# The first two blocks and the last make their output with w_out streaming past the activations; eight early chunks instead of ten; a new order of all operations

## The chip, the cores and the metric

One NeuronCore of a Trainium2 chip runs the program. The metric is device time in microseconds of one execution; a plain run's time and the span of the profiled execution are given side by side below.

## The reference, cut to what matters

A decayed linear attention over 4 batches, 8 heads, 768 tokens and head size 48 makes x (3072 tokens by 384), and a two-layer feed-forward with a cosine gate makes the output:

```python
for t in range(S):
    cur = np.einsum('bhd,bhe->bhde', u[None] * kt, vt)
    y[:, :, t] = np.einsum('bhd,bhde->bhe', rt, state + cur)
    state = w[None, :, :, None] * state + np.einsum('bhd,bhe->bhde', kt, vt)
x = y.transpose(0, 2, 1, 3).reshape(B * S, H * D)     # 3072 x 384
h = x @ w_in                                           # 3072 x 2048
g = h * np.cos(h)
out = g @ w_out                                        # 3072 x 384
```

## The kernel before

**Attention.** The tokens are cut into 24 chunks of 128 (six per batch). A chunk multiplies r and k by decay tables, makes scores, masks them, and multiplies by v and by the state of the chunk before. There are two forms. An *early* chunk transposes r and k on TensorE (`tr`, L970), makes scores (`mm_a`, L1089), the state product (`mm_z`, L1142) and x (`mm_x`, L1116 for the state's part and L1127 for the chunk's own). GpSimd (POOL) makes the product of r and k (L998), multiplies it by u (L1048) and decays k (L1006); VectorE (DVE) sums the products into `a` (L1054), masks (L1094) and splits x into a high and a low part (L1306); ScalarE (ACT) makes eight scaled diagonals from `a` (L1071). A *late* chunk has its transposes on DVE, stacks two half chunks and needs fewer matmuls (L1231, L1239, L1288). `EARLY = 10` says how many chunks take the early form.

**Feed-forward.** Six blocks of 512 tokens, and w_in's 2048 columns in 16 slices f, give 96 steps. A step is `h` (nine 512-column matmuls in a reduced fp32 format, high and low parts, L357), then on ACT and DVE in turn `qi` (L376), `rest` (L379), `cos` (L382), `gate` (L1399, writes h times cos back to PSUM), `gh` (L1402) and `gl` (L1405), then `o`: for each of three 128-wide parts of the output, three matmuls with a slice of w_out loaded as weights and the 512 tokens of gh or gl streaming (L373). The output so comes out transposed, three PSUM banks at a time, and DVE turns it back (L1431) into one SBUF tile `o` that is stored in pieces of 384 bytes (L1444, L1446). Blocks 0 and 1 take turns in groups of slices (`CUTS`), so that weights can be converted while they run; each group's end stores or adds to the output in DRAM (the adding DMA is issued by POOL). That makes twelve stored units: four for each of blocks 0 and 1, and one for each of the other four.

**Weights.** 32 pieces of w_in and w_out are read as 64-bit words and converted by ACT, DVE and POOL (L757, L765, L776, L787, L797, L804) during the first 170 us.

**Order.** Every operation is listed with its engine, a cost and the operations it waits for. `PLACE`, a table of numbers, gives each a rank; a planner walks the ranks with the costs and writes the instructions of each engine in the order that comes out. Where it sees a gap on TensorE ahead of the first `o`, it fills it with warm-up matmuls of 128 columns (L1462). Each engine's instructions run in that written order.

## Time and profile before

| | |
|---|---|
| Median of 3 runs | 500.93 us (500.54 to 501.88) |
| The profiled execution, its own time | 501.31 us |
| Its span in the profile | 499.5 us |
| TensorE (PE) busy | 486.6 us, 97% |
| VectorE (DVE) busy | 384.2 us, 77% |
| ScalarE (ACT) busy | 281.3 us, 56% |
| GpSimd (POOL) busy | 192.9 us, 39% |
| Share of the chain that ended last | PE 90%, DMA 3%, DVE 2% |

The span runs from the first to the last instruction that the profile recorded; the execution's own time is 1.8 us longer. PE counts as busy while any matmul is in its pipeline, and warm-up matmuls count as well, so 97% is not 97% of useful work.

### The profile page before, as it was taken

How to read it: one execution, taken by the hardware profiler on the slowest of the kernel's cores; microseconds unless marked ns; L12 is line 12 of the kernel's file. 1: busy time of each engine (PE TensorE's matmuls, PEld its weight loads, DVE VectorE, ACT ScalarE, POOL GpSimd, SP SyncE). 2: the span in 40 equal slices, each digit the busy share in tenths (PEclk: the TensorE clock that was granted, in tenths of full speed). 3: DMA queues.
4: the chain of work that ended last, by engine and by line, in shares of the span. 5: the costliest groups of instructions: out<-in, count | busy, mean ns of one | idle time of the engine just before them, and what ended most of it. 6: DMA issues, size and time to landing. Idle time of an engine off the chain costs nothing.

```text
span 499.5 us, 12059 instructions
## 1 busy us (share of the span) xinstructions
PE 486.6 (97%) x4676; PEld 393.8 (79%) x4676; DVE 384.2 (77%) x718; ACT 281.3 (56%) x644; POOL 192.9 (39%) x191
## 2 busy tenths in 40 slices
PE   9998999999999999999999999999999999999992
PEld 6887878878888878887878788887888888888881
DVE  6898999889899877777876895868857775665452
ACT  1987868566646655365565565565546545444440
POOL 6878342545756656543624242343505020000000
PEclk9999999999999999999999999999999999999998
DMA  7899647689897986477645466455533421110003
GB/s 140 172 186 171 140 140 193 155 143 156 147 207 113 184 109 118 62 169 141 132 115 141 126 143 145 132 128 142 130 77 92 142 80 33 33 31 2 1 0 70
DMA packets 150674, 59.19 MB, mean 118 GB/s; under 512 B 134223, under 2 KB 146513, under 8 KB 150609
## 3 DMA queue, kind: packets, MB, share of 16 engines
q1 hardware_dynamic: 136880, 53.24, 46.0%
q0 software_dynamic: 12672, 4.72, 9.8%
q8 instruction: 38, 0.62, 0.5%
q10 hardware_dynamic: 1056, 0.39, 0.3%
q14 instruction: 28, 0.22, 0.1%
HBM read 48.50 MB, written 9.44 MB: 116 GB/s over the span
## 4 chain that ended last, share of the span: by engine, by line
PE 90%; DMA 3%; DVE 2%; POOL 1%; SPq 1%; issue 1%; ACT 0%; DVEq 0%; POOLq 0%
PE psum L373 39%; PE psum L357 38%; PE psum L1288 3%; PE psum L1462 2%; PE psum L1231 2%; DMA out_dram<-o 1%; PE psum L1239 1%; DVE o L1431 1%; PE psum L1089 1%; PE psum L1127 1%; DMA early_v<-in_v_dram 1%; SPq L886 1%; PE psum L1116 1%; DMA early_k<-in_k_dram 1%; PE psum L970 1%
## 5 line engine op out<-in xcount | busy, mean ns | idle before, releaser
L373 PE MATMUL psum<-gh,w_out_hi 128*128 128x512 f32 x288 | 114.8, 399 | 0.9 <-DVE o L1431 0.9
L357 PE MATMUL psum<-xh,w_in_hi 128*128 128x512 f32 x288 | 114.1, 396 | 0.0
L357 PE MATMUL psum<-xh,w_in_lo 128*128 128x512 f32 x288 | 113.1, 393 | 0.0
L373 PE MATMUL psum<-gl,w_out_hi 128*128 128x512 f32 x288 | 113.1, 393 | 0.0
L373 PE MATMUL psum<-gh,w_out_lo 128*128 128x512 f32 x288 | 112.9, 392 | 0.0
L357 PE MATMUL psum<-xl,w_in_hi 128*128 128x512 f32 x288 | 112.7, 391 | 0.0
L1402 ACT CAST gh<-psum 128x512 fp32r<-128x512 f32 x96 | 56.0, 583 | 64.0 <-PE psum L373 33.8
L1405 DVE TENSOR_TENSOR gl<-psum,gh 128x512 fp32r<-128x512 f32 x96 | 65.6, 683 | 31.6 <-ACT gh L1402 30.9
L373 PEld LDWEIGHTS psum<-gh,w_out_hi 128*128 128x128 f32 x288 | 54.1, 188 | 14.5 <-DVE o L1431 0.9
L357 PEld LDWEIGHTS psum<-xh,w_in_hi 128*128 128x128 f32 x288 | 54.1, 188 | 13.1 <-issue 0.6
L373 PEld LDWEIGHTS psum<-gl,w_out_hi 128*128 128x128 f32 x288 | 54.1, 188 | 11.8
L357 PEld LDWEIGHTS psum<-xh,w_in_lo 128*128 128x128 f32 x288 | 54.1, 188 | 11.7
L357 PEld LDWEIGHTS psum<-xl,w_in_hi 128*128 128x128 f32 x288 | 54.1, 188 | 11.6
L373 PEld LDWEIGHTS psum<-gh,w_out_lo 128*128 128x128 f32 x288 | 54.1, 188 | 11.4 <-DVE w_out_lo L804 0.2
L1210 POOL TENSOR_TENSOR T<-T,k 48x512 f32<-48x512 f32 x28 | 37.2, 1328 | 55.5 <-ACT T L1196 29.0
L787 POOL TENSOR_TENSOR f<-f,raw 128x384 int32<-128x384 int32 x32 | 36.5, 1143 | 44.1 <-DVE f L776 26.3
L376 ACT ACTIVATE decT_r<-psum 128x512 int32<-128x512 f32 x41 | 24.5, 597 | 31.6 <-PE psum L357 31.4
L376 ACT ACTIVATE decT_k<-psum 128x512 int32<-128x512 f32 x41 | 24.4, 595 | 27.7 <-PE psum L357 26.9
L1196 ACT ACTIVATE T<-ident,a 128x128 f32<-128x128 f32 x112 | 37.1, 392 | 0.8 <-DVE a L1054 0.8
L1446 POOL DMA_DIRECT2D out_dram<-o x24 | 28.0, 1473 | 24.1 <-DVE o L1431 24.1
L379 DVE SCALAR_TENSOR_TENSOR decT_r<-psum,decT_r 128x512 f32<-128x512 f32 x41 | 28.0, 683 | 11.3 <-ACT decT_r L376 11.2
L379 DVE SCALAR_TENSOR_TENSOR decT_k<-psum,decT_k 128x512 f32<-128x512 f32 x41 | 28.0, 682 | 10.6 <-ACT decT_k L376 10.3
(161 smaller groups left out, 786.1 us busy)
## 6 DMA issues: line engine op xcount, KB each, us to landing
raw<-in_moe_w_out_dram SPq DMA_DIRECT2D x32, 384.0 KB, 3.5
raw<-in_moe_w_in_dram SPq DMA_DIRECT2D x32, 192.0 KB, 3.4
raw<-in_moe_w_in_dram SPq DMA_DIRECT2D x16, 384.0 KB, 3.8
out_dram<-o POOLq DMA_DIRECT2D x24, 192.0 KB, 5.3
raw<-in_k_dram SPq DMA_DIRECT2D x55, 80.0 KB, 3.0
raw<-in_r_dram SPq DMA_DIRECT2D x55, 80.0 KB, 2.4
out_dram<-o SPq DMA_DIRECT2D x22, 192.0 KB, 3.9
f<-in_k_dram SPq DMA_DIRECT2D x14, 192.0 KB, 3.6
```

The costliest lines, as they stand in the source:

```text
L357: nc.tensor.matmul(ph, a, b_, start=(i == 0), stop=(i == len(mm) - 1))
L373: nc.tensor.matmul(acc, a[:, ks], b_, start=(first and i == 0), stop=(last and i == 2))
L376: nc.scalar.activation(qi, ph, AF.Copy, scale=INV_2PI, bias=0.25)
L379: nc.vector.scalar_tensor_tensor(q, ph, INV_2PI, qi, op0=ALU.mult, op1=ALU.subtract)
L787: lambda: nc.gpsimd.tensor_tensor(ai(), ai(), cn(), op=ALU.add),
L1196: nc.scalar.activation(to, ident2[:, None, :].to_broadcast([P, 2, SUB]), AF.Copy, scale=ab()[:, h : h + 1])
L1210: nc.gpsimd.tensor_tensor(M_(n)[rows], by_head(rT)[rows], b_late[1]()[rows], op=ALU.mult)
L1231: nc.tensor.matmul(scores(n)[:, h, :], by_head(kT)[other(n), h, :], M_(n)[other(n), h, :], start=True, stop=True,)
L1288: nc.tensor.matmul(xv()[G * g : G * g + G, kk, tokens(n)], w_[rows, e0 : e0 + G], M_(n)[rows, h, :], start=g not in opened, stop=True, ski ...
L1402: nc.scalar.copy(gh(), ph())
L1405: nc.vector.tensor_tensor(gl(), ph(), f32(gh()), op=ALU.subtract)
L1446: nc.gpsimd.dma_start(dst, src, accum_op=ALU.add)
```

## The change

- For blocks 0 and 1 (`FLAT`) and for the last block, `o` is made the other way round: a 128-token slice of gh or gl is loaded as weights, and the 384 columns of w_out stream past. That is four tiles of three matmuls per step instead of three tiles of three. The output comes out with tokens in rows, so there is no transpose: ACT copies each finished tile (in the last block DVE and ACT in turn, and half of the last tile each), and it is stored in rows of 1536 bytes. The copies go to a ring `R_ob` of nine SBUF tiles instead of the single `o`.
- For blocks 0 and 1, `gate` writes to the SBUF tile q instead of PSUM, so gh and gl are made from SBUF, and h has two PSUM banks instead of three; the fourth accumulator takes the other.
- Eight early chunks instead of ten.
- A second pair of PSUM banks for the early transposes, a tile of its own for the mask `upper`, new costs for the planner, a new `PLACE`, and another count of warm-up matmuls.

```diff
-EARLY = 10
+EARLY = 8
 PLACE = (
-    14, 0, 7, 2, 3, 1, 12, 11, 6, 8, 5, 10, 15, 16, 24, 27, 40, 44, 22, 20, 28, 35, 13, 9, 31, 34, 25, 30, 33, 51, 42,
+    2, 0, 11, 3, 4, 5, 13, 21, 19, 9, 6, 12, 18, 20, 29, 37, 33, 36, 248, 7, 23, 26, 14, 10, 30, 27, 25, 46, 32, 57,
...
-        B_TR = [pair(0)]
+        B_TR = [pair(0), pair(6)]
...
+        FLAT = set(range(GRP))
+        R_ob = R_f + [Tile(t.ap[:, 0:DM], t.parts) for t in o_part]
...
-            ph, q, gh, gl = Buf(B_H), Buf(R_q), Buf(R_gh), Buf(R_gl)
+            flat_o, last = n in FLAT or n == NBLK - 1, n == NBLK - 1
+            ph, q, gh, gl = Buf(bank[3:5] if n in FLAT else B_H), Buf(R_q), Buf(R_gh), Buf(R_gl)
...
+            gb = q if n in FLAT else ph
+
+            def f_gate(ph=ph, q=q, gb=gb):
+                nc.vector.tensor_tensor(gb(), ph(), q(), op=ALU.mult)
...
-                acc_b[n, f0] = [Buf(B_ACC) for _ in range(NK)]
+                acc_b[n, f0] = [Buf([*B_ACC, bank[6 if last else 5]] if flat_o else B_ACC) for _ in range(nt if flat_o else NK)]
...
+                for t in range(nt):
+
+                    def o_(acc=acc[t], gh=gh, gl=gl, f=f, t=t, f0=f0, f1=f1):
+                        mm_o(acc()[:, 0:DM], gh(), gl(), f, t, f == f0, f == f1 - 1)
+
+                    oo = op(PE, s + 2.0 + 0.01 * t, 0.69, o_, [o6, (o7, 0.45), w_hi, (w_lo, 0.17)], [acc[t], gh, gl], line="o", mode=1)
+                    if f == f1 - 1:
+                        ob = Buf(R_ob)
+                        if not last:
+                            parts = ((ACT, SP if f0 == 0 else POOL, 0, 4),)
+                        elif t == nt - 1:
+                            parts = (DVE, SP, 0, 2), (ACT, ACT, 2, 4)
+                        else:
+                            parts = ((ACT if t % 2 else DVE, SP, 0, 4),)
...
-                    warm_up(int((o.gap - 0.1) / 0.057))
+                    cold = min(max(WARM_AT - (o.start - o.gap), 0.0), o.gap)
+                    warm_up(max(int(cold / 0.107 + (o.gap - cold - 0.1) / 0.057), 0))
```

`mm_o`, which was there for the fallback path, loads `a[:, ts]` (gh or gl) and streams `b_` (w_out):

```python
mm = ((g_hi, w_hi), (g_lo, w_hi), (g_hi, w_lo))
for i, (a, b_) in enumerate(mm):
    nc.tensor.matmul(acc, a[:, ts], b_, start=(first and i == 0), stop=(last and i == 2))
```

The new order moves instructions at three places that the prediction speaks of. The first is POOL near the program's start: the products r by k (L998, now L1007), the product by u (L1048, now L1057) and the decay of k (L1006, now L1015) of the first chunks. Before:

```order
L998 TENSOR_TENSOR f_109<-early_r_94,k_78 128x384
L998 TENSOR_TENSOR f_110<-early_r_95,k_77 128x384
L998 TENSOR_TENSOR f_105<-early_r_96,k_79 128x384
L1048 TENSOR_TENSOR f_110<-f_110,u_b 128x384
L1048 TENSOR_TENSOR f_105<-f_105,u_b 128x384
```

After:

```order
L1007 TENSOR_TENSOR f_110<-early_r_94,k_77 128x384
L1057 TENSOR_TENSOR f_110<-f_110,u_b 128x384
L1007 TENSOR_TENSOR f_105<-early_r_95,k_79 128x384
L1057 TENSOR_TENSOR f_105<-f_105,u_b 128x384
L1015 TENSOR_TENSOR k_79<-k_79,dec_k 128x2x4x48
```

The first chunk's product by u stood fourth, behind three products of r and k; it now stands second.

The second place is PE between the first `h` and the second (L357, now L362), where the early chunks' matmuls stand. Before, behind the first nine matmuls of h (the fourteen warm-ups L1462 and the rest are left out):

```order
L1142 MATMUL psum<-v_82,early_k_88 48x48 x8
L970 MATMUL psum<-ident,early_k_89 112x64 x8
...
L1089 MATMUL psum<-T 128x128 x8
L1116 MATMUL psum<-T,s 32x128 x16
L1127 MATMUL psum<-T,v_82 32x128 x16
L357 MATMUL psum<-xh,w_in_hi 128x512
L357 MATMUL psum<-xl,w_in_hi 128x512
```

After (L979, L1098, L1151, L1125 and L1136 are the new lines of tr, mm_a, mm_z and mm_x, and L369 is o in its new form):

```order
L1098 MATMUL psum<-T 128x128 x8
L979 MATMUL psum<-ident,early_k_90 112x64 x8
L979 MATMUL psum<-ident,early_r_97 112x64 x8
L369 MATMUL psum<-w_out_hi_68,gh_111 128x384
L369 MATMUL psum<-w_out_hi_68,gl_113 128x384
L369 MATMUL psum<-w_out_lo_69,gh_111 128x384
L1151 MATMUL psum<-early_v_91,early_k_90 48x48 x8
L362 MATMUL psum<-xh,w_in_hi 128x512
```

The first o now stands among the early chunks' matmuls, ahead of the second h; before, three more h stood ahead of the first o. Five early chunks' x (L1127) stood ahead of the first h before, four stand ahead of it now.

The third place is ACT at the end of the program, behind the last gh. Before:

```order
L1402 CAST gh_112<-psum 128x512
L1444 DMA out_dram<-o 32x16x96 x2
L1473 TENSOR_LOAD flag
```

After:

```order
L1414 CAST gh_112<-psum 128x512
L1436 COPY f_106<-psum 128x3x4x32
L1436 COPY f_108<-psum 128x3x2x32
L1447 DMA out_dram<-f_108 128x192
L1532 TENSOR_LOAD flag
```

ACT now copies the second tile and half of the fourth, and its store is one of half a tile (768 bytes a row); DVE copies the first, the third and the other half, and the three transposes that DVE had there are gone.

## Rows read from the trace of the kernel before

**Rows 1.** Windows: length, busy PE, PEld, DVE, ACT, POOL (instructions), clock, DMA, GB/s
```profile
0.00:8.43 8.43, 7.32 (x65) 5.27 (x66) 6.66 (x37) 1.49 (x2) 4.43 (x18) 1.00 0.64 119
8.43:20.00 11.57, 11.57 (x220) 9.76 (x220) 7.35 (x14) 6.83 (x22) 11.45 (x12) 1.00 0.90 179
20.00:56.98 36.98, 35.10 (x876) 29.64 (x870) 34.03 (x70) 31.49 (x90) 23.75 (x26) 1.00 0.95 172
56.98:107.12 50.14, 50.10 (x275) 40.26 (x271) 45.59 (x87) 34.44 (x72) 22.92 (x21) 1.00 0.69 161
109.47:490.50 381.03, 381.02 (x3254) 308.44 (x3254) 287.49 (x509) 206.45 (x459) 130.35 (x117) 1.00 0.51 106
```

**Rows 2.** Windows of the warm-up matmuls alone (L1462): PE and weight loads
```profile
0.00:20.00 20.00, 9.40 (x129) 8.37 (x129) 1.00 0.79 154
20.00:56.98 36.98, 1.52 (x21) 1.18 (x21) 1.00 0.95 172
```

**Rows 3.** Chain that ended last, from 408 us: start, us, what
```profile
412.68 1.93 PE psum L1288 x128
...
449.84 2.06 PE psum L373 x9
```

**Rows 4.** Timeline: start, us, engine, line: a change of matmul kind, and four transposes
```profile
414.54 0.19 PEld L373 LDWEIGHTS psum<-gh,w_out_hi 128*128 128x128 f32 x1
414.54 0.50 PE L373 MATMUL psum<-gh,w_out_hi 128*128 128x512 f32 x1
...
414.88 0.40 PE L373 MATMUL psum<-gh,w_out_lo 128*128 128x512 f32 x1
...
12.16 0.66 PE L590 MATMUL psum<-ident,decT_k 128*128 128x128 f32 x4
```

**Rows 5.** Chain from 44 us: one early chunk's five pieces, first and last
```profile
48.68 0.66 PE psum L970 x16
...
51.88 1.09 PE psum L1089 x16
```

**Rows 6.** Timeline of PE from 404.8 us: the first half of a late chunk
```profile
405.83 0.27 PE L1231 MATMUL psum<-T 48*64 48x64 f32 x2
...
406.91 0.50 PE L373 MATMUL psum<-gh,w_out_hi 128*128 128x512 f32 x1
```

**Rows 7.** Timeline near the start; in brackets idle time before, and what ended it
```profile
7.98 3.60 POOL L998 TENSOR_TENSOR f<-early_r,k 128x384 f32<-128x384 f32 x3 [2.93 <-DMA k<-in_k_dram]
...
13.48 1.00 DVE L1054 TENSOR_REDUCE a<-f 128x8 f32<-128x384 f32 x2
```

**Rows 8.** Timeline at 107 us, and PE's waits from 60 to 130 us
```profile
107.04 0.72 DVE L1431 STREAM_TRANSPOSE o<-psum 128x512 f32<-128x512 f32 x1 [1.76 <-DMA out_dram<-o]
...
PE psum L373 <- DVE o L1431: 0.9, 2, 0.5
```

**Rows 9.** Timeline at the end, and DMA issues there (median us to landing)
```profile
489.16 2.09 DVE L1431 STREAM_TRANSPOSE o<-psum 128x512 f32<-128x512 f32 x3 [1.67 <-PE psum L373]
490.10 0.39 PE L373 MATMUL psum<-gl,w_out_hi 128*128 128x512 f32 x1
491.28 0.98 ACTq L1444 DMA_DIRECT2D out_dram<-o  x2
...
out_dram<-o ACTq DMA_DIRECT2D x2, 192.0 KB, 5.2
```

**Rows 10.** Stores of out over the program, and a copy of 384 columns from PSUM
```profile
DMA to landing us min/median/max: 2.6/4.4/7.4
...
L594 ACT COPY dec_k<-psum x1: 482/482/482, 12.9 to 12.9; 128x384 f32<-128x384 f32 x1
```

**Rows 11.** Groups by line: two pieces of a step's chain
```profile
L376 ACT ACTIVATE decT_r<-psum 128x512 int32<-128x512 f32 x41 | 24.5, 597 | 31.6 <-PE psum L357 31.4
...
L379 DVE SCALAR_TENSOR_TENSOR decT_r<-psum,decT_r 128x512 f32<-128x512 f32 x41 | 28.0, 683 | 11.3 <-ACT decT_r L376 11.2
```

**Rows 12.** One line's instructions (ns min/median/max): w_in's low part, both operands in SBUF
```profile
L804 DVE TENSOR_TENSOR w_in_lo<-f,w_in_hi x16: 537/550/953, 33.7 to 157.3; 128x384 fp32r<-128x384 f32 x16
```

More of the change, by code (lines that the diff above doesn't have):

```diff
@@ L450 @@
         b_up = Buf(o_part[:1])
-        upper = o_room[:, 0:C].bitcast(I32)
+        upper = att.tile([P, C], I32, name="upper")
         warm = o_room[:, C : 2 * C].bitcast(BF16)[:, 0:P]
@@ L1438, with st @@
                 for a in range(P // G):
-                    def st(a=a, ob=ob, row=row, f0=f0, by=nc.scalar if last and a % 2 else nc.sync):
+                    def st(a=a, ob=ob, row=row, f0=f0):
                         dst = out[row : row + TB, a * NK * G : (a + 1) * NK * G].rearrange("(b i) e -> i b e", i=G)
```

108 lines of the change are left out of this document (68 added, 40 removed), and 192 rows, old and new, of the table PLACE.

## The prediction, made before the changed kernel was run

> **What bounds the kernel now.** I read the windows first, because they tell where TensorE (PE) has no room left. From 57 to 490 us it is busy in all but 0.04 of 50.14 us and 0.01 of 381.03 us of two long stretches, at a granted clock of 1.00, the upper of its two levels, 2.4 GHz [rows 1]; the 2.4 us between these two hold a wait, to which I come. So from 57 us on the time is the sum of PE's work, and only less work on PE makes it shorter. Before 57 us it is otherwise. The warm-up matmuls, which compute nothing, take 9.4 us of the first 20 and 1.5 of the next 37 [rows 2], and PE stands idle for 1.1 and 1.9 more, so some 14 of the first 57 us do no work. From 20 to 57 us VectorE (DVE) is busy 34.0 of 37.0 us: there DVE sets the pace. From 8.4 to 20 us it is busy only 7.35 of 11.57, waiting for its inputs, so that the start is held by the chain from the loads through GpSimd (POOL). After the last matmul, 490.10 + 0.39 = 490.49 us, the span of 499.5 us has 9.0 us left without PE [rows 9]. Three things can thus be gained or lost: work per matmul from 57 us on, the first 57 us, and the tail.
>
> **The change part by part.** The sum is made against the profiled execution, 501.31 us, with its span of 499.5.
>
> *The tail.* Now three transposes follow one another, the last ending at 489.16 + 2.09 = 491.25, four stores go out from 491.28, and the median to landing of those on ScalarE's queue is 5.2 us; the second on it goes out half of 0.98 us later, so the last lands at about 497, and 2.5 us remain to the span's end [rows 9]. The new form finishes its tiles one after another, so three of four are copied and two stored while PE still works. After the last matmul come half a copy, a store and the same 2.5 us. A copy of 384 columns takes 0.48 us [rows 10]; half takes between 0.24 and 0.48, I take 0.35. The half tile on SP stands behind another store on its queue, 0.1 to 0.4 us with the handing over; I take 0.2. A store landed in 2.6 us at the quickest and 4.4 at the median, for twice the bytes and among other traffic [rows 10]; alone I take 2.6. That is 5.65 us for 9.0: **-3.4** (bounds -3.9 and -1.5, the latter with the median store).
>
> *Two chunks late instead of early.* One early chunk's five pieces stand in a row in the chain from 48.68 to 51.88 + 1.09 = 52.97 us: 4.29 us [rows 5]. A late chunk's first half takes 406.91 - 405.83 = 1.08 us [rows 6]; the second half of two chunks takes 1.93, or 0.97 each [rows 3]. A late chunk also breaks into the stream of step matmuls twice, four changes of kind: a first matmul lasts 0.50 us where the next lasts 0.40 [rows 4], so 0.1 each. Together 2.45 us. Two chunks: 2 x (2.45 - 4.29) = **-3.7** (-3.0 if the early pieces overlap better elsewhere, -4.1 without the changes).
>
> *The new form of o.* Both forms stream 4608 columns per step, in nine matmuls of 512 or twelve of 384. Nine take 2.06 us, 0.229 each [rows 3]. At 2.4 GHz 512 columns stream in 0.213 us, which leaves 0.016 per instruction; 384 then take 0.160 + 0.016 = 0.176, twelve 2.11, and the 48 steps of the three blocks lose 48 x 0.05 = **+2.4**. If time went purely with columns it would be 0. The other bound is the weight load, busy 0.19 us [rows 4] and now longer than the streaming that hides it: 12 x 0.19 = 2.28, or +10.6 over 48 steps. I take the lower value, since four fp32 loads of 128 columns and their matmuls fit in 0.66 us, at most 0.165 each [rows 4]: a load can follow a load in less than 0.176.
> The Trainium skill, page "TensorE: Matmul & The Clock Gate", section "The mechanism", says that a weight load overlaps a running matmul only when the row groups differ, which would lay every load here open. The trace disagrees for this kernel: full-height loads sit beside full-height matmuls and the pair still comes every 0.229 us.
>
> *The start.* POOL makes three products of r and k from 7.98 us on (3.60 us), then the products by u, and DVE's first sum `a` starts at 13.48 [rows 7]; diagonals, masks and x follow from it. In the new order the first u product stands second, so the first sum can start after about 1.2 + 1.0 us, 3.3 us sooner. The first transposes no longer stand behind 57 warm-ups. Further, four chunks instead of five stand ahead of the first h and o starts among the early chunks, so PE has step work where it stood in warm-ups or idle in 20 to 57 us, 1.5 + 1.9 us [rows 1, 2]; I give 2.2 of it back. Together **-5.5**. Bounds: -2 if loads or a TensorE clock that rises later, for want of those warm-ups, hold the chain; -8 if the 14 lost us shrink to 6, which is little more than the time to the first loaded chunk.
>
> *The single output tile.* At 107 us the transposes of one unit wait 1.76 us for the stores of the unit before, since both use `o`, and PE waits 0.9 us for them in two pieces, each with a fresh weight load, 0.1 to 0.2 us, behind it [rows 8]. Nine tiles instead of one remove it: **-1.2** (0 if another wait takes its place). The 24 transposes of blocks 0 and 1 leave DVE, and 32 copies of 0.48 us join ScalarE, which has room (34.4 of 50.1 us busy [rows 1]): nothing on PE's path.
>
> *New waits.* gl of blocks 0 and 1 now reads two SBUF operands. The line that does so today, w_in's low part, has a median of 0.550 us, a minimum of 0.537 and a maximum of 0.953 [rows 12], so now and then it waits for something, 0.4 us at most; 32 gl would lose 0 to 13 us of DVE time, about 0.4 at the typical excess.
> The Trainium skill, page "SBUF: State Buffer", section "SBUF: two separate sides", names it: a DVE instruction with two SBUF inputs and a GpSimd instruction exclude each other for a whole instruction. The trace agrees in kind, and its order keeps it rare; if gl met POOL at random, DVE would lose many us in its busiest stretch.
> Two h banks instead of three leave less room for lateness (rival below). I put +1.5 for new waits altogether (0 to +6).
>
> *Sum:* -3.4 - 3.7 + 2.4 - 5.5 - 1.2 + 1.5 = -9.9, so 491.4 for an execution like the profiled one, and **491.0** against the median of 500.93, which lies 0.38 lower.
>
> **The rivals.**
> *The start stays.* From 20 us on DVE is 92% busy and the DMA share is 0.95 [rows 1]; if the loads or DVE's total hold the early chunks, the start gives nothing: 491.0 + 5.5 = 496.5. Against it: the hole of 4.2 us in DVE from 8.4 to 20.
> *Weight loads show.* At 0.19 us per load o costs +10.6 instead of +2.4: 499.2. Against it: the four loads within 0.66 us.
> *Slower: h runs out of banks.* With two banks, h of a step waits for gate of the step two before. Between h's end and that moment PE has one h and two o, 2.06 + 2 x 2.11 = 6.3 us; qi, rest, cos and gate need 0.60 + 0.68 and about as much again, 2.6 us [rows 11], plus handing over. DVE must therefore never be late by more than some 3.5 us. It is 91% busy from 57 to 107 us [rows 1]. If the 32 steps of blocks 0 and 1 lose more than 9.9 / 32 = 0.31 us each, the kernel is slower; at 0.45 each beyond what I put, 491.0 + 14.4 = 505.4. Against it: with three banks PE now waits there almost never, and the early chunks that made DVE full are fewer.
> *All goes well.* No new waits and -8 at the start: 491.0 - 1.5 - 2.5 = 487.0.
>
> **How the numbers follow.** My forecast has 0.55, the start that stays 0.19, visible weight loads 0.07, too few banks 0.08, all well 0.11. The predicted time is the forecast's, 491.0. The range, 486 to 498, holds the forecast with its bounds, all well and the start that stays; visible loads and too few banks lie beyond it. A measurement of this kernel tells 0.3%, 1.5 us, from no change. Faster by more: forecast, start, all well, and most of the loads' case, 0.88; within: 0.05, from the rest of the loads' case and milder bank trouble; slower: 0.07.
>
> **What would show it.** Right: a second h well before 57 us and no stretch from 25 us on with warm-ups; a first sum `a` near 10 us; twelve matmuls of o in 2.1 us; the span ending 5.5 to 6 us after the last matmul; no wait of PE for the copies. Wrong: 0.19 us or more between the 384-column matmuls; PE waiting for gate or gl between 50 and 180 us; a first h no earlier than 36.9 us.

## The result and the profile after

The changed kernel took 506.36 us, the median of 9 runs (504.45 to 509.25), beside 502.00 us for 9 runs of the kernel before (500.54 to 503.37). The ratio is 1.0102, 95% interval 1.0074 to 1.0130: one per cent slower, where 491.0 was forecast and 498 was the range's upper end. Its profiled execution took 508.35 us with a span of 506.6, against 501.31 and 499.5 before, so the traces differ by 7.0 us and these are what I account for. The medians differ by 4.4 us: the profiled execution of the changed kernel is 2.0 us slower than its median, so 2.7 of the 7.0 us belong to this pair of executions.

The windows of the changed kernel, columns as in [rows 1]:

```profile
20.00:56.98 36.98, 33.48 (x717) 26.89 (x709) 32.52 (x60) 27.09 (x75) 23.88 (x25) 1.00 0.71 150
57.00:200.00 143.00, 137.75 (x1114) 119.65 (x1115) 130.00 (x209) 97.84 (x214) 82.24 (x76) 0.99 0.73 158
59.75:63.16 3.41, 3.41 (x10) 2.85 (x9) 2.17 (x6) 1.90 (x5) 1.01 (x1) 0.50 0.02 5
```

The kernel before in the longest of these windows:

```profile
57.00:200.00 143.00, 142.08 (x892) 114.04 (x888) 126.44 (x229) 88.85 (x186) 77.74 (x71) 1.00 0.78 150
```

Between 57 and 200 us PE stood idle for 0.92 us before and stands idle for 5.25 now. The rest of the span tells nothing of this size. I counted the matmuls of each kind in each stretch, times the spacing of that kind where PE runs undisturbed (0.229 us for 512 columns, 0.175 for 384); the pieces of a chunk count with 4.29 us for an early one [rows 5] and about 2.3 for a late one. What a stretch has beyond that is time without counted work: warm-ups, waits, a low clock. The ledger in us, good to a few tenths:

| | before | after | difference |
|---|---|---|---|
| counted work of PE | 470.4 | 468.3 | -2.1 |
| without work, to 57 us | 10.7 | 14.7 | +4.0 |
| without work, 57 to 200 us | 3.5 | 10.2 | +6.6 |
| without work, 200 us to the last matmul | 4.6 | 5.3 | +0.7 |
| behind the last matmul | 9.1 | 6.9 | -2.2 |

The five differences add up to 7.0; the 1.2 us ahead of the first matmul are in neither column. How far the steps have come shows in the windows of `h` alone (L357 before, L362 now; nine matmuls a step). Before:

```profile
0.00:57.00 57.00, 2.37 (x10) 1.63 (x10) 1.00 0.89 165
113.40:200.00 86.60, 43.94 (x180) 33.17 (x178) 1.00 0.85 148
```

After:

```profile
0.00:57.00 57.00, 4.69 (x18) 3.27 (x18) 1.00 0.84 154
113.40:200.00 86.60, 43.21 (x171) 31.25 (x171) 1.00 0.74 146
```

At 57 us the new kernel is ahead, two steps against one; its first h begins at 32.45 us, before at 36.93. From 113.4 to 200 us it makes 19 steps where the kernel before made 20.

**The start.** The first sum `a` starts at 10.34 us instead of 13.48. But the warm-ups are in the way. The windows of the warm-ups alone, after and then before:

```profile
8.10:10.60 2.50, 2.50 (x25) 2.48 (x24) 1.00 1.34 170
```

```profile
4.10:6.40 2.30, 2.30 (x23) 2.30 (x23) 1.00 0.94 178
6.50:8.40 1.90, 1.90 (x36) 1.82 (x33) 1.00 0.87 158
```

The clock column says 1.00 throughout here, since the trace records no clock before 6.4 us in the kernel before and 12.0 us in the changed one, but the same instruction comes every 0.100 us up to 6.4 us in the kernel before and every 0.053 behind that: the two levels, 1.2 and 2.4 GHz. In the changed kernel it still comes every 0.100 us at 10.6. PE in the timeline after:

```profile
8.00 2.85 PE L1520 MATMUL psum<-o 128*128 128x128 bf16 x25
11.49 1.18 PE L1520 MATMUL psum<-o 128*128 128x128 bf16 x14
12.60 0.44 PE L979 MATMUL psum<-ident,k 64*112 64x64 f32 x8
```

The second chunk's k had landed by 10.65 us, when POOL began its product; its transposes stand behind 39 warm-ups until 12.60.

**From 50 to 60 us.** POOL, DVE and PE in the timeline:

```profile
52.36 1.00 POOL L1005 TENSOR_TENSOR f<-f,f 128x384 f32<-128x384 f32 x1
52.42 1.36 DVE L813 TENSOR_TENSOR w_out_lo<-f,w_out_hi 128x384 fp32r<-128x384 f32 x1
53.44 1.20 POOL L1057 TENSOR_TENSOR f<-f,u_b 128x384 f32<-128x384 f32 x1
53.70 1.35 DVE L785 SCALAR_TENSOR_TENSOR f<-raw,f 128x384 int32<-128x384 int32 x1
56.15 0.99 POOL L1013 TENSOR_TENSOR f<-f,dec_k 128x384 f32<-128x384 f32 x1
56.25 1.30 DVE L813 TENSOR_TENSOR w_out_lo<-f,w_out_hi 128x384 fp32r<-128x384 f32 x1
57.48 0.55 DVE L1315 TENSOR_TENSOR xl<-psum,xh 128x384 fp32r<-128x384 f32 x1
58.08 0.44 PE L369 MATMUL psum<-w_out_hi,gh 128*128 128x384 f32 x1 [3.27 <-DVE xl L1315]
```

Both converting operations, 0.55 us elsewhere (L813 in [rows 12]; L785 has a median of 0.551), take 1.3 here, beside GpSimd's products of a late chunk (L1005, L1057, L1013), and the low part of an early chunk's x stands behind them. The fourth tile of o needs the bank that this x holds, and waits 3.27 us. Behind this wait the granted clock is 0.50 from 59.75 to 63.16 us, as the windows show: 1.2 GHz for 3.41 us, some 1.7 us of work.

Not every execution has this. Here L1005 begins 0.06 us ahead of the first L813. In the trace of the sixteenth experiment below, whose edit touches nothing ahead of 86 us, the first L813 (51.81) and the L785 (52.28) begin ahead of L1005 (52.44) and take 0.55 us each, PE waits 1.2 us instead of 3.3, the third h begins at 56.35 us instead of 58.71, and the clock does not fall. Of the changed kernel's nine runs two have a mean granted clock of 0.997 and 0.998, against 0.994 in the profiled one; they took 506.07 and 504.45 us, still more than the kernel before.

**From 103 to 109 us.** POOL, DVE and PE in the timeline:

```profile
104.39 1.01 DVE L785 SCALAR_TENSOR_TENSOR f<-raw,f 128x384 int32<-128x384 int32 x2
105.02 1.27 POOL L796 TENSOR_TENSOR f<-f,raw 128x384 int32<-128x384 int32 x1
106.23 0.89 POOL L1445 DMA_DIRECT2D out_dram<-o  x1
106.64 1.96 DVE L813 TENSOR_TENSOR w_out_lo<-f,w_out_hi 128x384 fp32r<-128x384 f32 x1
106.82 1.35 POOL L796 TENSOR_TENSOR f<-f,raw 128x384 int32<-128x384 int32 x1
106.89 0.51 PE L362 MATMUL psum<-xh,w_in_hi 128*128 128x512 f32 x1 [0.57 <-ACT w_in_hi L806]
108.52 0.54 DVE L813 TENSOR_TENSOR w_in_lo<-f,w_in_hi 128x384 fp32r<-128x384 f32 x1
109.12 0.50 PE L362 MATMUL psum<-xh,w_in_lo 128*128 128x512 f32 x1 [1.50 <-DVE w_in_lo L813]
```

POOL adds the words of a weight piece between the adding stores that it issues. DVE's w_out_lo begins at 106.64, while POOL works, and takes 1.96 us instead of 0.55; w_in_lo stands behind it, and PE waits 1.50 us for that, after 0.57 us for the high part. No store held the word of that high part: it was added from 105.02 on, less than 0.1 us behind the first of the two L785, which ended at 104.94. The second addition could have run from 105.40, when the second L785 ended; it began at 106.82, behind the first one (to 106.29) and the issue of a store.

The groups by line say how often DVE's instructions with two SBUF operands stand still like this:

```profile
L1417 DVE TENSOR_TENSOR gl<-psum,gh 128x512 fp32r<-128x512 f32 x64 | 43.9, 686 | 37.1 <-ACT gh L1414 36.5
L1417 DVE TENSOR_TENSOR gl<-o,gh 128x512 fp32r<-128x512 f32 x13 | 13.0, 1002 | 0.9 <-ACT gh L1414 0.9
L1417 DVE TENSOR_TENSOR gl<-decT_r,gh 128x512 fp32r<-128x512 f32 x9 | 11.9, 1318 | 0.9 <-ACT gh L1414 0.9
L1417 DVE TENSOR_TENSOR gl<-decT_k,gh 128x512 fp32r<-128x512 f32 x10 | 8.5, 847 | 1.2 <-ACT gh L1414 1.0
L813 DVE TENSOR_TENSOR w_out_lo<-f,w_out_hi 128x384 fp32r<-128x384 f32 x16 | 13.6, 851 | 0.1
```

gl from PSUM takes 0.686 us. The 32 from SBUF take 33.4 us together; 32 x 0.686 is 22.0, so they stand still for 11.4 us. The conversions L813 (13.6 here, 10.3 for w_in_lo) have 23.9 - 32 x 0.55 = 6.3 us of it, before 0.5. The longest one:

```profile
195.22 1.29 POOL L1219 TENSOR_TENSOR T<-T,k 48x512 f32<-48x512 f32 x1
196.27 3.61 DVE L1417 TENSOR_TENSOR gl<-decT_r,gh 128x512 fp32r<-128x512 f32 x1
196.47 0.83 POOL L1445 DMA_DIRECT2D out_dram<-o  x1
197.08 2.24 POOL L1013 TENSOR_TENSOR f<-f,dec_k 128x384 f32<-128x384 f32 x2
```

It lasted through three tensor instructions of GpSimd and the issue of a store, until 199.88. The issue alone does not do this: four low parts L813 that met nothing but the issue of stores (at 86.93, 88.02, 89.06 and 152.62 us) lasted 0.52 to 0.55 us.

The planner knew of such meetings. The code marks these gl (`port=n in FLAT`), the converting and GpSimd's tensor instructions, and lets no two marked ones overlap in its plan. But it writes only the order of each engine; in the run the engines drifted apart from the planned times.

**The tail**, against [rows 9], timeline and DMA issues:

```profile
499.36 0.34 PE L369 MATMUL psum<-w_out_lo,gh 128*128 128x384 f32 x1
499.74 0.36 DVE L1438 COPY f<-psum 128x192 f32<-128x192 f32 x1
500.13 0.32 ACT L1436 COPY f<-psum 128x192 f32<-128x192 f32 x1 [0.97 <-DVE f L1438]
...
out_dram<-f ACTq DMA_DIRECT2D x1, 96.0 KB, 3.7
```

The two half copies came one after the other, and the last store landed in 3.7 us.

### The profile page after: what moved, and what is told of

Its sections match the earlier page's. It is cut to its first block, busy times and chain, and to the rows that moved or that the text cites. A ratio compares the mean times of both kernels' runs of the same rounds, so it can differ in the third digit from the quotient of the medians.

```text
span 506.6 us, 12297 instructions
## 1 busy us (share of the span) xinstructions
PE 488.3 (96%) x4790; PEld 408.4 (81%) x4790; DVE 392.2 (77%) x698; ACT 293.4 (58%) x676; POOL 201.2 (40%) x197
## 4 chain that ended last, share of the span: by engine, by line
PE 76%; DVE 13%; ACT 3%; DMA 3%; issue 2%; SPq 1%; POOL 1%; DVEq 0%; ACTq 0%
PE psum L362 33%; PE psum L378 20%; PE psum L369 13%; DVE gl L1417 3%; PE psum L1297 3%; PE psum L1240 2%; DVE w_out_lo L813 2%; DVE f L785 1%; DVE w_in_lo L813 1%; PE psum L1248 1%; DVE f L774 1%; DMA out_dram<-o 1%; PE psum L1098 1%; PE psum L1136 1%; DMA raw<-in_moe_w_in_dram 1%
## 5 line engine op out<-in xcount | busy, mean ns | idle before, releaser
L362 PE MATMUL psum<-xh,w_in_lo 128*128 128x512 f32 x288 | 114.1, 396 | 2.8 <-DVE w_in_lo L813 2.8
L362 PE MATMUL psum<-xh,w_in_hi 128*128 128x512 f32 x288 | 114.6, 398 | 1.0 <-ACT w_in_hi L806 0.6
L362 PE MATMUL psum<-xl,w_in_hi 128*128 128x512 f32 x288 | 113.5, 394 | 0.0
L369 PE MATMUL psum<-w_out_hi,gh 128*128 128x384 f32 x192 | 65.7, 342 | 3.6 <-DVE xl L1315 3.3
L362 PEld LDWEIGHTS psum<-xh,w_in_lo 128*128 128x128 f32 x288 | 54.4, 189 | 15.5 <-DVE w_in_lo L813 4.1
L362 PEld LDWEIGHTS psum<-xh,w_in_hi 128*128 128x128 f32 x288 | 54.2, 188 | 13.6 <-ACT w_in_hi L806 0.9
L369 PE MATMUL psum<-w_out_hi,gl 128*128 128x384 f32 x192 | 65.0, 338 | 0.0
L369 PE MATMUL psum<-w_out_lo,gh 128*128 128x384 f32 x192 | 64.7, 337 | 0.0
L362 PEld LDWEIGHTS psum<-xl,w_in_hi 128*128 128x128 f32 x288 | 54.4, 189 | 10.9 <-DVE xl L1315 0.4
L378 PE MATMUL psum<-gh,w_out_hi 128*128 128x512 f32 x144 | 58.2, 404 | 0.0
L378 PE MATMUL psum<-gl,w_out_hi 128*128 128x512 f32 x144 | 56.7, 393 | 0.0
L796 POOL TENSOR_TENSOR f<-f,raw 128x384 int32<-128x384 int32 x32 | 36.0, 1127 | 51.7 <-DVE f L785 19.2
L378 PE MATMUL psum<-gh,w_out_lo 128*128 128x512 f32 x144 | 56.4, 392 | 0.0
L369 PEld LDWEIGHTS psum<-w_out_hi,gh 128*128 128x128 f32 x192 | 36.3, 189 | 6.5 <-DVE xl L1315 3.6
L369 PEld LDWEIGHTS psum<-w_out_hi,gl 128*128 128x128 f32 x192 | 36.2, 188 | 2.0 <-DVE gl L1417 0.3
L369 PEld LDWEIGHTS psum<-w_out_lo,gh 128*128 128x128 f32 x192 | 36.2, 188 | 0.0
L997 POOL TENSOR_TENSOR T<-T,k 112x512 f32<-112x512 f32 x16 | 21.7, 1358 | 28.6 <-DVE T L991 20.4
```

The lines of the kernel that those rows point to most:

```text
L362: nc.tensor.matmul(ph, a, b_, start=(i == 0), stop=(i == len(mm) - 1))
L369: nc.tensor.matmul(acc, a[:, ts], b_, start=(first and i == 0), stop=(last and i == 2))
L378: nc.tensor.matmul(acc, a[:, ks], b_, start=(first and i == 0), stop=(last and i == 2))
L796: lambda: nc.gpsimd.tensor_tensor(ai(), ai(), cn(), op=ALU.add),
L997: nc.gpsimd.tensor_tensor(t, t, b_late[0]()[0:KP], op=ALU.mult)
```

## The experiments

Every time stands beside runs of the kernel before on the same chip; n is the number of runs, and the last numbers are the ratio to those runs with its 95% interval (the changed kernel: 1.0102). The runs of one kernel scatter by several us, and a trace shows one of them: the traces of the seventh, eleventh, sixteenth and seventeenth experiment are of executions 1.8 to 2.8 us quicker than their medians, that of the changed kernel of one 2.0 us slower, so idle times from two traces can overstate what an edit gave.

**First: which part of the change costs.** Each of these takes one part away from the new kernel, or adds one to the old. In the first, gl of blocks 0 and 1 reads unused PSUM columns instead of the gate in SBUF.

```diff
-    nc.vector.tensor_tensor(gl(), gb(), f32(gh()), op=ALU.subtract)
+    src = gb() if gb is ph else psum[:, 2:3, DM:512].to_broadcast([P, 4, P])
+    nc.vector.tensor_tensor(gl() if gb is ph else gl().rearrange('q (a b) -> q a b', a=4), src, ...
```

> The changed kernel, except that gl of blocks 0 and 1 takes its first operand from 512 elements of PSUM that lie unused beside an accumulator, instead of from the gate in SBUF; the gate is still made and gh still copied from it, so this leaves the true low part out of gl. Order and banks stay. Contention theory (gl, with two SBUF operands, stands still while POOL works, 11.7 us in 57 to 200 us, and makes DVE late): mean gl of blocks 0 and 1 back from 0.98 to about 0.68 us, PE's waits from 100 to 200 us (4.9 us) mostly gone, 4 to 8 us faster than the changed kernel, so 498 to 502 us. Bank theory (two h banks): the waits stay, 505 to 508 us. Start theory (the wait of 3.3 us at 55 us and the fall of the clock behind it): that wait stays and so does the time, within 1.5 us of 506.4, since gl is slow mostly later.

Measured: 508.78 us (505.87 to 509.86, n 4), 1.0118 [1.007, 1.0166]. gl was quick again, but PE now waited for it, a row that the new kernel does not have (waits of PE, 40 to 200 us):

```profile
PE psum L369 <- DVE gl L1418: 3.0, 3, 1.9
```

These columns lie in a bank in which o is summed, so gl and o waited for each other (gl for o 2.1 us). The edit put a wait in the place of the one that it took away, and decides nothing.

In the second, the kernel before gets gl from two SBUF operands in blocks 0 and 1 and nothing else.

```diff
-    nc.vector.tensor_tensor(gl(), ph(), f32(gh()), op=ALU.subtract)
+    nc.vector.tensor_tensor(gl(), f32(gh()) if n < GRP else ph(), f32(gh()), op=ALU.subtract)
```

> The kernel before, except that gl of blocks 0 and 1 reads gh twice, two SBUF operands, instead of the gate in PSUM and gh; it leaves the true low part out of gl. Order, banks and the form of o stay as before. Contention theory: some of these 32 gl stand still beside POOL, as in the changed kernel, mean 0.9 to 1.1 us instead of 0.68; DVE loses about 10 us from 57 to 200 us, of which it had 16 free, so 3 to 9 us slower, 505 to 511 us. Bank theory and start theory: no change, 502 us within 1.5.

Measured: 505.34 us (504.42 to 506.62, n 7), 1.0075 [1.0053, 1.0098]: 3.5 us slower by the medians, 3.8 by the ratio. The group by line and the window:

```profile
L1405 DVE TENSOR_TENSOR gl<-gh 128x512 fp32r<-128x512 f32 x32 | 28.4, 888 | 2.6 <-ACT gh L1402 2.6
...
57.00:200.00 143.00, 138.77 (x867) 109.80 (x866) 131.14 (x223) 85.05 (x177) 80.99 (x71) 1.00 0.76 147
```

32 instructions that lasted 0.2 us longer on the mean, 6.5 us of DVE time, took 3.3 us from PE between 57 and 200 us. This one operand, which I had priced at 0.4 us, costs the old kernel most of what the new one lost there.

In the third, h of blocks 0 and 1 may also use the two attention banks.

```diff
-    ph = Buf(bank[3:5] if n in FLAT else B_H)
+    ph = Buf([*bank[3:5], *B_ATT] if n in FLAT else B_H)
```

> The changed kernel, except that h of blocks 0 and 1 may also take the two PSUM banks of the late chunks when they are free (10 of 32 steps do). The order of instructions stays. Bank theory: PE's waits from 57 to 200 us shrink by half or more, 3 to 6 us faster than the changed kernel, 500 to 503 us. Contention theory and start theory: PE waits for the conversions and for DVE, not for a bank, so 506.4 us within 1.5.

Measured: 506.72 us (506.44 to 509.51, n 4), 1.0108 [1.0066, 1.015]: as the changed kernel, and PE stood idle for 4.9 us between 57 and 200 instead of 5.25. Nor does any wait of PE for a bank of h stand in the changed kernel's trace. The rival of too few banks falls.

In the fourth, the kernel before gets the last block alone in the new form, with its own order otherwise; the code of `out_copy` and of the four tiles is that of the change.

```diff
+            last = n == NBLK - 1
...
+            if last:
+                def out_copy(t, by, a0, a1, ob, acc=acc):
...
+                    oo = op(PE, s + 2.0 + 0.01 * t, 0.69, o_, [o6, (o7, 0.45), w_hi, (w_lo, 0.17)], [acc[t], gh, gl], line="o", mode=1)
...
-    b_fine = Buf(bank[6:7])
+    b_fine = Buf(bank[7:8])
```

> The kernel before with the last block alone in the new form (w_out moving, tiles of 128 tokens copied by ACT and DVE and stored whole). As predicted: tail 3.4 us shorter, 16 steps 0.05 us longer each, together -2.6, so 499.4 us. By the tail that the changed kernel's profile shows (6.9 us behind the last matmul instead of 9.1) it would be -2.2 + 0.8 = -1.4, so 500.6 us. If the last block were what makes the changed kernel slow: 504 us or more.

Measured: 500.35 us (499.31 to 501.26, n 10) beside 501.85, 0.9966 [0.9949, 0.9982]: 1.5 us faster than the kernel before, and the fastest version found that leaves nothing out. Its last matmul ends 6.74 us ahead of the span's end, 2.3 less than in [rows 9], and 16 steps lose 16 x 0.05 = 0.8; the sum of the two is the 1.5 measured.

**Second: the start, and GpSimd's additions.** With `WARM_AT` at 12 the planner counts on the low clock up to 12 us and puts fewer warm-ups there.

```diff
-WARM_AT = 6.4
+WARM_AT = 12.0
```

> The changed kernel with WARM_AT = 12 instead of 6.4: fewer warm-ups ahead of the transposes of k and r of the second chunk (in the changed kernel's profile 39 warm-ups, most of them at 1.2 GHz and 0.107 us apart, stand from 8.0 to 12.6 us ahead of these transposes, whose k had landed by 10.65 us). Start theory: the transposes come 1.5 to 1.9 us sooner, the first scores at about 13 instead of 14.7 us, and the time falls by as much, 504.0 to 505.0 us. Pace theory (from 20 to 200 us the converting of the weights and the order on VectorE set the pace, and TensorE waits for them): the scores come sooner, but the time stays, 506.4 us within 1.

Measured: 505.54 us (501.07 to 507.86, n 7), 1.0040 [0.9999, 1.008]. The second chunk's transposes start at 10.86 us instead of 12.60 and the first h at 30.70 instead of 32.45; the wait for x at 55 us stayed (3.1 us). 1.7 us at the start became 0.8 at the end by the medians, within the scatter; by the ratios, 1.0040 against 1.0102, it is some 3. Two of the seven runs took 501.07 and 501.84 us, the others 505.00 to 507.86, so how much it gives stays open.

The next changes the place of two matmuls, so that the bank that the warm-ups write is opened first and they begin at 3 us.

```diff
-    2, 0, 11, 3, 4, 5, 13, 21, 19, 9, 6, 12,
+    2, 0, 11, 3, 4, 5, 13, 6, 19, 9, 21, 12,
```

> The changed kernel with two of the six bank-opening matmuls exchanged, so that the bank of the warm-ups is opened first and 7 warm-ups fill the wait of 0.9 us at 3.0 us; nothing else moves. Start theory: TensorE is then busy without a break from 1.2 to 6.7 us, the clock rises at 6 to 8 us instead of 12.0, the 39 warm-ups take 2.3 instead of 4 us, the first scores come 1.5 us or more sooner, 504 to 505 us. Pace theory: the clock rises earlier, the time stays, 506.4 us within 1. If the clock's rise has to do with something other than the break, it stays at 12 us and so does the time.

Measured: 507.62 us (501.29 to 509.67, n 10), 1.0073 [1.0037, 1.011]. The clock did rise earlier, and was lost again; windows of that kernel:

```profile
4.60:8.00 3.40, 2.43 (x33) 1.64 (x33) 3.06 (x12) 0.48 (x1) 1.94 (x5) 1.00 1.02 172
8.00:11.40 3.40, 3.40 (x32) 3.33 (x29) 2.38 (x5) 1.13 (x4) 2.29 (x2) 0.50 1.23 174
```

PE had waited 0.97 us for k until 6.62. From 55.79 us on the clock was low again, for 6.83 us, twice as long as in the changed kernel. So this start gained nothing in the median; two of the ten runs took 501.29 and 502.44 us.

The next cuts GpSimd's add in the converting of weights (L796) from 384 columns to one; the one behind it does the same to the kernel before.

```diff
-    lambda: nc.gpsimd.tensor_tensor(ai(), ai(), cn(), op=ALU.add),
+    lambda: nc.gpsimd.tensor_tensor(ai()[:, 0:1], ai()[:, 0:1], cn()[:, 0:1], op=ALU.add),
```

> The changed kernel with GpSimd's addition in the converting of the weights cut from 384 columns to one, in all 32 pieces; it leaves out the low words of the other columns. It takes about 1 us of GpSimd and of the chain of each piece, and most of what can stand in the way of VectorE's instructions with two SBUF operands. Pace theory: TensorE's waits from 57 to 200 us, 6.6 us more than before, go for the most part, gl falls from 0.98 to below 0.8 us, and the time falls by 4 to 8 us, 498 to 502 us. Start theory: the waits at the start stay, and with them most of the loss, 504 to 506.5 us.

Measured: 501.48 us (499.22 to 502.68, n 10), 0.9984 [0.9965, 1.0003].

> The kernel before with the same addition cut to one column. Pace theory: before, TensorE waited only about 1 us from 57 to 200 us, so little is there to win, 500.5 to 502 us; what the changed kernel wins more than this is what its converting costs it. If the converting set the pace of the kernel before as well, 498 us or less.

Measured: 501.86 us (500.73 to 504.93, n 10), 0.9998 [0.9975, 1.0021]. The additions cost the kernel before nothing and the changed one all that it lost. The window of the changed kernel without them:

```profile
57.00:200.00 143.00, 142.29 (x1213) 125.25 (x1212) 129.41 (x217) 101.41 (x223) 63.98 (x79) 1.00 0.75 161
```

POOL is busy 18 us less, DVE only 0.6, and PE's idle time falls from 5.25 to 0.71 us.

**Third: DVE's order, DVE's work, and the old form.** The ranks of six operations are changed so that at 51 to 58 us the two x low parts and gate come ahead of the conversions; two places of the table:

```diff
-    201, 219, 209, 237, 176, 204, 249, 251, 82, 129, 155, 170,
+    201, 219, 209, 237, 176, 204, 249, 244.2, 82, 129, 155, 170,
...
-    217, 247, 255, 259, 262, 265, 269, 270,
+    217, 247, 244.4, 259, 246.5, 265, 263.9, 270,
...
```

> The changed kernel with another order on VectorE at 51 to 58 us alone: the low parts of x, rest and gate of the second step and its gl stand ahead of the converting instructions that they stood behind, and the two copies to wN come later. Start theory: the wait of 3.3 us at 55 us and the fall of the clock behind it (1.3 us) go and do not come back, 4 to 5 us faster than the changed kernel, 501.5 to 502.5 us. Pace theory: the third h starts about 3 us sooner than at 58.7 us, but TensorE then waits sooner and longer for gl and for converted weights, so that at most 2 us are left, 504.5 to 506.5 us.

Measured: 507.4 us (506.29 to 507.87, n 4), 1.0104 [1.0068, 1.014]. The third h began at 54.5 us instead of 58.7, and the total did not move. The timeline shows where the 4 us went (L826 is the add, L843 the low parts):

```profile
103.71 1.96 DVE L843 TENSOR_TENSOR w_out_lo<-f,w_out_hi 128x384 fp32r<-128x384 f32 x1
103.89 1.35 POOL L826 TENSOR_TENSOR f<-f,raw 128x384 int32<-128x384 int32 x1
106.19 0.80 PE L392 MATMUL psum<-xh,w_in_lo 128*128 128x512 f32 x1 [1.50 <-DVE w_in_lo L843]
106.78 0.63 PE L392 MATMUL psum<-xh,w_in_hi 128*128 128x512 f32 x1
107.20 0.63 PE L392 MATMUL psum<-xl,w_in_hi 128*128 128x512 f32 x1
```

The same collision, 3 us earlier, with the same 1.96 and 1.50 us; behind the wait a matmul comes every 0.42 us, the low clock, which this order has here and not at 59 us. Of 4.2 us, 1.5 were left twelve steps later (113.4 to 111.9, the start of the fifteenth h), and none in the medians.

In the next, FLAT is empty, so that blocks 0 and 1 have the old form, with ranks derived from the new table.

```diff
-    FLAT = set(range(GRP))
+    FLAT = set()
```

> The changed kernel with blocks 0 and 1 in the old form of o (FLAT empty: three h banks, gate in PSUM, three accumulators, transposes on VectorE into the single tile o); the start, eight early chunks and the last block stay as changed, and the ranks of the new copies are given to the transposes. The o of 32 steps takes 1.6 us less. If the new form of blocks 0 and 1 (SBUF gate, 32 copies on ScalarE, two banks) makes the 6 us of waits from 57 to 200 us: 498 to 501 us. Pace theory: VectorE has 24 transposes (17 us) more and 11 us of standing still less, the converting stays as late, and the time stays, 503 to 508 us.

Measured: 545.83 us (543.91 to 546.2, n 4), 1.0859. The derived order does not fit this form (PE waits 12.6 us for gl between 40 and 200 us); inconclusive.

In the next, DVE's sign instruction in the converting (L785) is cut to one column.

```diff
-    ai(), hw(), -0x40000000, ai(), op0=ALU.bitwise_and, op1=ALU.bitwise_or
+    ai()[:, 0:1], hw()[:, 0:1], -0x40000000, ai()[:, 0:1], op0=ALU.bitwise_and, op1=ALU.bitwise_or
```

> The changed kernel with one of VectorE's three instructions per converted piece of weights (the one that puts sign and exponent in, 0.57 us) cut from 384 columns to one; it leaves these bits out, so the weights are wrong. It takes 0.5 us of VectorE and of the chain from each of 32 pieces, 15 us in all, and leaves GpSimd's additions. Pace theory with VectorE as the engine that is late: 3 to 6 us faster than the changed kernel, 500 to 503 us, about as much as cutting the additions gave (4.9 us). If it was GpSimd's place in the chain that counted there, not VectorE: less than 2 us, 504.5 to 506.5 us.

Measured: 506.98 us (504.16 to 507.79, n 5), 1.0103 [1.0069, 1.0137]. DVE is busy 122.75 us between 57 and 200 instead of 130.00, and nothing is gained in the median. So it is not DVE's busy time alone.

The next writes 21 of the 32 gates to PSUM columns beside the accumulators, with the two edits of the order and of `WARM_AT` above.

```diff
+    R_side = [Tile(psum[:, 0:4, DM:512], side[0:4])]
+    gb = Buf(R_side) if on_side else q if n in FLAT else ph
```

> A version meant to be faster: the changed kernel, with gate of 21 of the 32 steps of blocks 0 and 1 written to the 4 x 128 columns of PSUM that stand unused beside the four accumulators (banks 0 to 3, h in 4 and 5), so that their gl reads PSUM; with the order of VectorE at 51 to 58 us as in the run before the last but two, and with WARM_AT = 12. If the three causes add up (wait at 55 us 4.5, gl's standing still 2 to 4, warm-ups 1): 497 to 500 us. Pace theory: what one gives is taken back by the next wait for converted weights, 503 to 506 us.

Measured: 534.8 us (533.51 to 537.25, n 4), 1.0668. PE's o waits 9.6 us for gates: as in the first experiment the bank ties them together, and nothing follows for the cause.

**Fourth: combinations, and other work of GpSimd.** The order with x first, together with the cut additions, and together with gl from PSUM:

> The changed kernel with both: VectorE's order at 51 to 58 us with the low parts of x, rest and gate ahead of the converting, and GpSimd's additions cut to one column (this leaves out the low words of the weights). The additions alone gave 501.5 us. If the wait at 55 us is a loss of its own beside the late converting: 497 to 499.5 us. If the converting decides and the wait is only where it shows first: 500.5 to 502.5 us.

Measured: 500.73 us (499.95 to 505.14, n 10), 0.9996 [0.9971, 1.0021].

> The changed kernel with VectorE's order at 51 to 58 us as before and, at once, gl of blocks 0 and 1 reading unused PSUM columns instead of the gate in SBUF (this leaves the true low part out of gl). Each alone gave nothing (507.4 and 508.8 us). If the two mask one another, the wait at 55 us handing its time to gl's standing still and the other way round: 501 to 503.5 us. If GpSimd's queue decides: 505 to 508 us.

Measured: 507.36 us (506.38 to 507.83, n 4), 1.0108 [1.0068, 1.0147], with 3.7 us of PE's waits for gl, as in the first experiment. With the additions cut the better order is worth 0.8 us at most, within the scatter.

The next two cut other work of GpSimd. First its products (L997, L1005, L1013, L1057) for the two chunks that became late.

```diff
+    if i < 10:
+        nc.gpsimd.tensor_tensor(mb()[:, 0:1], rb()[:, 0:1], kb()[:, 0:1], op=ALU.mult)
+        return
```

> The changed kernel with GpSimd's products of the first two late chunks alone (decay of k transposed, r by k, by u, decay of k; about 4.3 us each chunk, on GpSimd between 56 and 125 us) cut to one head or column; it leaves these products out of two chunks. These are two of the four late chunks that stand ahead of block 2 now, where two stood before. If the work that the two more late chunks put on GpSimd in the converting stretch is what makes it late: 2 to 4 us faster than the changed kernel, 502.5 to 504.5 us. If it is the additions themselves, in the way of VectorE or in the chain: 505.5 to 507.5 us.

Measured: 504.25 us (502.61 to 505.51, n 10), 1.0047 [1.0023, 1.007]. What went is the wait at 55 us, 0.8 us instead of 3.3: the first L813 and the L785 take 0.55 us there, and xl begins at 55.23 instead of 57.48. The waits for w_in_lo stayed at 2.8 us. But the sixteenth experiment's trace has only 1.2 us at 55 us with these products in place, so how much of the 2 us is theirs is not shown.

Then the 24 adding stores of blocks 0 and 1.

```diff
-    return lambda: nc.gpsimd.dma_start(out[r0 : r0 + C, cols], ob()[:, cols], accum_op=ALU.add)
+    return lambda: None
```

> The changed kernel without the 24 adding stores of blocks 0 and 1 that GpSimd issues (about 1 us each on its queue, 19 us from 57 to 200 us, and waits of up to 4.3 us for copies on ScalarE); it leaves the sums over three of four groups of slices out of the output of these blocks. If GpSimd's queue is late because of its length and its waits: 2 to 5 us faster, 501.5 to 504.5 us. If what counts is GpSimd standing in VectorE's way in SBUF: 505 to 507.5 us.

Measured: 502.26 us (499.49 to 504.55, n 10), 1.0008 [0.9982, 1.0033]. The same place in its timeline, and its window:

```profile
100.53 2.23 POOL L796 TENSOR_TENSOR f<-f,raw 128x384 int32<-128x384 int32 x2 [1.70 <-DVE f L785]
102.09 1.08 DVE L813 TENSOR_TENSOR w_out_lo<-f,w_out_hi 128x384 fp32r<-128x384 f32 x1
103.70 0.50 PE L362 MATMUL psum<-xh,w_in_lo 128*128 128x512 f32 x1 [0.54 <-DVE w_in_lo L813]
...
57.00:200.00 143.00, 141.92 (x1210) 125.07 (x1210) 128.36 (x216) 101.43 (x222) 69.71 (x60) 1.00 0.55 136
```

Without the stores the two additions run one behind the other, w_out_lo loses 0.5 us instead of 1.4, PE waits 0.54 instead of 1.50, and its idle time in the window is 1.08 us. This edit also takes DMA traffic away (the DMA share falls from 0.73 to 0.55), and neither it nor the one before was made on the kernel before, which issues 24 adding stores too.

**Fifth: gl from one operand.** In blocks 0 and 1 gl is gh times a constant, one SBUF operand; the last run adds the order with x first.

```diff
     if gb is ph:
         nc.vector.tensor_tensor(gl(), gb(), f32(gh()), op=ALU.subtract)
+    else:
+        nc.vector.tensor_scalar(gl(), f32(gh()), 2.0**-12, None, op0=ALU.mult)
```

> The changed kernel, except that gl of blocks 0 and 1 is made from gh alone (gh times a constant, one SBUF operand, no PSUM); this leaves the true low part out of gl. It waits for gh as before, and no buffer or bank changes. The converting instruction with one SBUF operand stands still little (0.40 us instead of 0.35), so gl should fall from 1.07 us to 0.45 to 0.7, and VectorE's standing still from 21 to about 9 us between 30 and 200 us. If that standing still is the cause: 3 to 5 us faster than the changed kernel, 501.5 to 503.5 us, like the runs without GpSimd's additions (501.5) or adding stores (502.3), which cut it to 13.8 and 11.9 us. If GpSimd's own queue is the cause: 505.5 to 507.5 us.

Measured: 506.84 us (501.8 to 507.84, n 8), 1.0089 [1.0066, 1.0112]. This form did not escape; all instances of the line, ns min/median/max:

```profile
L1420 DVE TENSOR_SCALAR gl<-gh x32: 378/428/3347, 41.4 to 201.0; 128x512 fp32r<-128x512 f32 x32
```

They take 22.4 us together, 8.7 more than 32 medians, and the low parts L813, at 0.836 and 0.784 us on the mean, stand still for 8.3 us: 17.0 together, against 17.7 in the changed kernel. The standing still moved from one line to the other.

> The same with VectorE's order at 51 to 58 us of the run in which the low parts of x stood first (it too leaves the true low part out of gl). That order alone gave nothing, and 0.8 us beside the cut additions. If the wait at 55 us is only where late work shows first: within 1.5 us of the run with gl from one operand alone. If it is a loss of its own once VectorE is no longer late: 3 us or more faster than that, 500 us or less.

Measured: 504.93 us (503.11 to 506.74, n 12), 1.0052 [1.0035, 1.0069]. Quicker gl and the better order together give 1.4 us. The order alone gives 1.9 us beside the run before, between the two cases that were expected.

## Why the prediction was wrong

**The step that failed first, and by most, is "the start", -5.5.** It came out at +4.0. Its first part was right: the first sum came at 10.34 us, where "near 10" was foreseen. What I had as the lower bound, "a TensorE clock that rises later, for want of those warm-ups", happened, and the 39 warm-ups that remained, at the low level, held the second chunk by 1.7 us (the fifth experiment). The first h came 4.5 us sooner, hardly more than the one early chunk fewer ahead of it is worth (4.29 [rows 5]), so the sooner first sum was lost by then. Up to 57 us the warm-ups fell from 10.9 to 7.6 us, as foreseen, but PE's idle time behind its first matmul rose from 1.9 to 5.0 us, where I had counted on less of it; 4.2 us more are counted work that went more slowly or overlapped less, and no run shows why.
The largest wait is that at 55 us: early chunks and o side by side, as I had wanted, tied x, its bank and o together on a DVE that stretched conversions held up, beside the products of a chunk that had become late. Some 2 us of it are this execution's, since 1.2 us stand there in another. Mending the start gave little at the end: of 4.2 us the ninth experiment kept 1.5 at the fifteenth h and nothing in the median, and what the fifth gives is open. What stands ahead of PE at 104 to 109 us is the converted weights: with the third h 4.2 us sooner, w_in_lo began 2.9 us sooner (105.58 instead of 108.52), and PE waited the same 1.50 us for it. I had read the bound of 20 to 57 us from DVE's busy share, and took it for granted that time won there is kept.

**The second step that failed is "new waits", +1.5.** It came out at +6.6 between 57 and 200 us, above its bound of +6: 4.3 more of PE's idle time, 1.7 at the low clock, 0.6 that I did not trace. The mechanism was among those that I named, the size was wrong. I priced the second SBUF operand by w_in's low part, 0.550 at the median and 0.953 at most, and called 0.4 us typical. That row was read from an order in which these instructions seldom met GpSimd's. The new gl meets them often in spite of the plan: the far bound, 13 us of DVE time, was the right one (11.4 measured), and 6.3 more fell on the conversions, which I had not priced at all. The way to PE was another too: I named PE waiting for gate or gl as a sign, and it waited for x and for converted weights. The second experiment shows the price of the operand alone on the kernel before, 3.5 us.
The Trainium skill, page "SBUF — State Buffer", section "Who interferes with whom", says that a VectorE instruction with two SBUF inputs contends with a GpSimd instruction that reads SBUF, and that tensor_scalar can enter a mode that takes the same ports. The traces agree with both: gl at up to 3.61 us, and the form with one operand at up to 3.35.

**What GpSimd does there is the other half of it.** Cutting its additions brings the time back to that of the kernel before and the same cut on that kernel gives nothing; cutting the adding stores brings back about as much; cutting the products of two late chunks brings about 2 us. Cutting DVE's work or reordering DVE alone brings nothing. So the loss is shown to hang on GpSimd's work, most of it between 50 and 200 us, in a kernel that now has SBUF operands in its DVE stream.
Not settled is how it divides: GpSimd's own queue delays the additions (a store's issue between the two at 106.3 us) and with them the loads that wait for a buffer, and its tensor instructions keep DVE standing still (the 1.50 us at 109.1). The adding stores act through the queue, or through the DMA traffic, since their issue alone was not seen to hold DVE. Every cut of GpSimd's work eases both; the experiments that aimed at DVE alone either tied a PSUM bank or moved the standing still to other lines.

**Two chunks late, -3.7, and the new form of o, +2.4**, stand together in the counted work: -2.1 where -1.3 was predicted. By the spacings o costs +1.9 (576 matmuls at 0.175 us for 432 at 0.229), which leaves -4.0 for the chunks. My bound of -4.1 without the changes of kind was worked out wrongly: 2 x (2.05 - 4.29) is -4.5. The matmuls of 384 columns come every 0.17 to 0.18 us, as worked out, and no weight load shows. But the trade was costed on PE alone: the two chunks' products moved into the converting stretch on GpSimd, which the fifteenth experiment prices at about 2 us at most.

**The tail, -3.4**, was right in mechanism and measured -2.2, with -2.3 in the fourth experiment. Two parts were too small: the halves were copied one after the other, and the last store landed in 3.7 us where I took 2.6.

**The single output tile, -1.2**: its wait is gone, as foreseen, but PE waits 1.5 + 0.6 us at the same place for weights. The bound "0 if another wait takes its place" held.

Of the rivals, the slower one named the wrong mechanism: the banks of h (the third experiment), not the SBUF operand. The start that stays would have given 496.5; a start that loses was no case of mine.

## What to carry to other kernels

An instruction's median tells its price in the company that its order gave it; if an edit puts the same kind of operand into a stream that meets another engine, ask how busy that engine is in that stretch (GpSimd 82 of 143 us here), go by the far bound, and price too whatever stands behind it in order. A plan that keeps such instructions apart holds only as long as its times do. Count moved work on every engine that gets some of it, not only on the one that bounds. Time won ahead of a stage is kept only if the stage's own supply comes earlier too, so ask what paces the next gate before crediting it; here a single safe part of the change, the last block, was worth more than the whole.

## What the runs showed of the hardware

A DVE instruction with two SBUF operands that meets GpSimd can stand still through several of its tensor instructions: 3.61 us for a gl of 0.69, beside three of them and the issue of a store. Beside the issue of a store alone, four low parts lasted no longer than elsewhere (0.52 to 0.55 us).

Which of two instructions comes first decides much: with GpSimd's product 0.06 us ahead, DVE's conversion took 1.36 us, and with the conversion ahead 0.55.

The clock fell to 1.2 GHz for 3.41 us behind a wait of PE of 3.27 us that ended at 58.08 us. It also fell in the ninth experiment, at 105.78 us, within a wait of 1.50 us, and in the sixth, at 8.00 us, behind a wait of 0.97 us; behind the wait of 1.50 us at 109 us in the changed kernel it did not fall.
